# Gate and up products of the last two token blocks as seven row-tiled products for two column groups of both blocks, with another order of the FFN part

## The chip, the cores and the metric

The kernel runs on one core of one Trainium2 chip. The metric is the device time of one execution in microseconds. The core has TensorE (PE; PEld are its weight loads), VectorE (DVE), ScalarE (ACT), GpSimd (POOL) and SyncE (SP, which here issues nearly all DMAs); each works through its own queue in order.

## The reference

The input x is 2048 tokens of 640 numbers in bf16. It is normalised, and the result goes through an attention part (32 heads of 192, the last 512 keys) and a gated FFN of 1536 columns; the two are combined.

```
def _B_ref(x, w_gate, w_up, w_down):
    g = _silu(x @ w_gate)
    u = x @ w_up
    return (g * u) @ w_down

xn = _layernorm(x, axis=-1)
s = _A_ref(xn, A_k_cache, A_v_cache, A_wq, A_wo)
g = _silu(_B_ref(xn, B_w_gate, B_w_up, B_w_down))
return x + s * g
```

The change concerns `_B_ref`: the two products with `w_gate` and `w_up`, and when the third is made.

## The kernel before

The order of all instructions is written out by hand (`tc.manual_schedule()`); an engine executes its instructions in the order in which the program names them, and semaphores are put where data or buffers ask for them.

**Sizes.** P = 128. The tokens are four blocks (b) of 512 columns, the model width 640 is NC = 5 chunks of 128, and the FFN width 1536 is NF = 12 column groups (f) of 128. `xnT` holds the normalised input transposed, 128 x 5 x 2048, and `hT[b]` the hidden values of a block, 128 x 12 x 512; two `hT` buffers take turns.

**Gate and up** (`ffn_hidden`, L394, L401, L402). For each b and f, `hidden_mm` makes two groups of five matmuls of 128 x 512: gate into one bank and up into the other of a tile of `sc_tile()`. ACT then makes `sg` = Silu(gate), and DVE `hT` = up * `sg`. `sc_pool` has two such tiles, so the group f + 2 waits for the `hT` of f.

**Down** (`ffn_down`, L455 and L461). The product with `w_down` is made for two pairs of 128 token rows in a block (u = 0, 1) by Winograd's form of Strassen's seven products: the left operand is split into two halves of rows and of columns, `wd_sum` makes four sums of the weights, `sums` four sums of `hT` (S1 to S4). Each product is six matmuls of 128 x 320. Products 1, 6, 7 and 4 accumulate in one bank one after the other, and before each next one ACT or DVE has to have read the bank. In the blocks b = 1 to 3 one step of the down products of block b - 1 follows each group of gate and up; those of block 3 stand behind the blocks, between six products of the attention's q (`q_full`, L522).

**Around it.** The row blocks of x come by `load_x` on SP. Blocks 0 and 1 take their mean and variance from DVE (`ln_stats`), 2 and 3 from ACT (`ln_sums`, L357 and L361: two passes with an accumulator, one in the middle of the block before); `ln_apply` on DVE and a transposing DMA on SP (L385) fill `xnT`. Block 2 also holds the first loads of the attention (`load_k`, `transpose_k`, `load_wq`, `sum_k`) and the sums of x (`swap_x`, `combine_x`, L542) that the attention's q products use; block 3 `centre_k` and more of these. The attention starts with `scores` (L789).

**Row tiling.** The q products of the attention (`products`, L732, and `q_rows`, L720) already use it: each matmul takes 64 of the 128 rows of the array, `lo` or `hi`, and writes its own bank of a tile, so that ten matmuls of 64 x 512 do for two products of half the depth:

```
for c in range(NC):
    for h, r in enumerate((lo, hi)):
        nc.tensor.matmul(
            ps[:, h, :], ws[h][r, c, :], xs[h][r, c, :],
            start=(first and c == 0), stop=(c == NC - 1), skip_group_check=True,
        )
```

Of the kernel before, what the change touches and what calls it, by code (L numbers as in the profile page):

```python
# [15 lines left out]
def kernel(  # L16
# [144 lines left out]
    def copy_wq(pr, js):  # L161

        for j in js:
            nc.vector.tensor_copy(out=slot_of(w_all, full, *weights_of(pr, j)), in_=blocks_of(full, 0, j))
# [95 lines left out]
    with ExitStack() as fctx:  # L260
        ffa = fctx.enter_context(tc.tile_pool(name="ffa", bufs=3, side="right"))
        ffw = fctx.enter_context(tc.tile_pool(name="ffw", bufs=1, side="right"))
        lnw = fctx.enter_context(tc.tile_pool(name="lnw", bufs=4, side="right"))
        lnx = fctx.enter_context(tc.tile_pool(name="lnx", bufs=8, side="right"))
# [9 lines left out]
        junk = ffw.tile([P, D], bf, name="junk")  # L274

        def load_x(t, engs=(nc.sync,)):
            x_t[t] = lnx.tile([P, D], bf, name="x_t")
            n = P // len(engs)
            for k, eng in enumerate(engs):
                r = slice(k * n, (k + 1) * n)  # L280
                eng.dma_start(out=x_t[t][r, :], in_=x2[t * P + r.start : t * P + r.stop, :])
# [68 lines left out]
        def ln_sums(t, squares):  # L350

            b, ti = divmod(t, 4)
            if b not in ln:
                ln[b] = [lnw.tile([P, 8], f32, name="mv"), lnw.tile([P, 4], f32, name="rstd")]
            mv = ln[b][0]
            if not squares:
                nc.scalar.activation(junk[:], x_t[t][:], ACT.Identity, accum_out=mv[:, ti : ti + 1])  # L357
                if ti == 3:
                    nc.gpsimd.tensor_scalar(mv[:, 0:4], mv[:, 0:4], -1.0 / D, None, op0=ALU.mult)
            else:  # L360
                nc.scalar.activation(  # L361
                    junk[:], x_t[t][:], ACT.Square, bias=mv[:, ti : ti + 1],
                    accum_out=mv[:, 4 + ti : 5 + ti],
                )
# [7 lines left out]
        def ln_apply(t, parts=(slice(0, D),)):  # L372
            b, ti = divmod(t, 4)
            mv, rstd = ln[b]
            xns[t] = lnx.tile([P, D], bf, name="xn", bufs=4)
            if b == 0:
                nc.vector.reciprocal(rstd[:, t : t + 1], rstd[:, t : t + 1])
            for cols in parts:
                nc.vector.tensor_scalar(
                    xns[t][:, cols], x_t[t][:, cols], mv[:, ti, 0:1] if b < 2 else mv[:, ti : ti + 1],  # L380
                    rstd[:, ti : ti + 1], op0=ALU.subtract if b < 2 else ALU.add, op1=ALU.mult,
                )

        def ln_transpose_dma(t):
            nc.sync.dma_start_transpose(  # L385
                out=xnT[:, 0:NC, t * P : (t + 1) * P], in_=xns.pop(t)[:]
            )
# [54 lines left out]
        def ffn_down(b, u):  # L442

            if not down_banks:
                down_banks.extend(t[:, n, 0:HC] for t in (mm_tile(), mm_tile()) for n in range(2))
            U, V, W = (down_banks[k] for k in ((0, 2, 3), (1, 3, 2))[u])
            g = {}

            def a(side, k):
                rows = slice((u + 2 * side) * P, (u + 2 * side + 1) * P)  # L450
                return hTs[b][:, k * KD : (k + 1) * KD, rows]
# [8 lines left out]
            def total(to, x, y, op=ALU.add):  # L460
                nc.vector.tensor_tensor(to, x, y, op)  # L461

# [6 lines left out]
            def sums():  # L469
                total(S1, a(1, 0), a(1, 1))  # L470
                total(S2, S1, a(0, 0), ALU.subtract)

            def w1():
                for side in range(2):
                    g[side] = ffa.tile([P, D], bf, name="g_t", bufs=2)
                mm(W1, a(0, 0), U)
                nc.scalar.copy(p1, U)
                if (b, u) != (NB - 1, 0):
                    sums()
# [5 lines left out]
            def w6():  # L485
                mm(W6, S2, U, False)
                nc.scalar.copy(u2, U)
                gate(0, 0, p1)
                total(S3, a(0, 0), a(1, 0), ALU.subtract)

            def w5_():
                mm(W5, S1, W)
                nc.scalar.copy(w5, W)
                total(S4, a(0, 1), S2, ALU.subtract)

            def w7():
                mm(W7, S3, U, False)
                total(w5, U, w5)

            def w3():  # L500
                mm(W3, S4, W, False)
                total(u2, W, u2)
                gate(1, 1, w5)

            def w4():
                mm(W4, a(1, 1), U, False)
                gate(1, 0, U)
                store(1)

# [4 lines left out]
            if (b, u) == (NB - 1, 0):  # L514
                sums()
            return [w1, w2, w6, w5_, w7, w3, w4], rest

# [38 lines left out]

        hTs[0] = ffh.tile([P, NF, 512], bf, name="hT")
# [51 lines left out]
        xwork = []  # L609

        for b in range(NB):
            if b:
                hTs[b] = ffh.tile([P, NF, 512], bf, name="hT")
            nx = b + 1 < NB
            for f in range(NF):
                if nx and b and f == 0:
                    for t in range(4 * b + 4, 4 * b + 8):
                        load_x(t)
                if b or f >= 4:
                    ffn_hidden(b, f)  # L620
                if b == 0 and f >= 8:
                    wd_sum(f - 8)
                elif b:
                    if f == 0:
                        downs, rest = ffn_down(b - 1, 0)
                    elif f == 6:
                        rest()
                        downs, rest = ffn_down(b - 1, 1)
                    for _ in range(2 if f % 6 == 5 else 1):
                        downs.pop(0)()  # L630
                if nx and 2 <= f < 6:
                    if b == 0:
                        ln_stats(4 * b + 2 + f)
                    else:
                        for t in range(2 * (f % 2), 2 * (f % 2) + 2):
                            ln_sums(4 * b + 4 + t, f > 3)
                    if f == 5:
                        ln_rstd(b + 1)
                if nx and f in (6, 7):
                    for t in range(4 * b + 2 * f - 8, 4 * b + 2 * f - 6):  # L640
                        ln_apply(t)
                        ln_transpose_dma(t)
                if b == 2 and f == 0:
                    for half in range(2):
                        swap_x(DIFF[0], half, half)
                elif b == 2 and f == 8:
                    swap_x(DIAG, 0, 0)
                    xwork += x_combinations(DIFF[0]) + x_combinations(SUM[0])
                elif b == 3 and f == 0:
                    for half in range(2):  # L650
                        swap_x(DIFF[1], half, 2 + half)
                    swap_x(DIAG, 1, 3)
                elif b == 3 and f == 2:
                    xwork += [
                        u for to in (SUM[1], DIFF[1], DIAG) for u in x_combinations(to)
                    ]
                if xwork and (b == 2 or f % 2 == 0):
                    xwork.pop(0)()

                if b and f == NF - 1:  # L660
                    rest()
                if b == 2:
                    if f == 0:
                        load_k(0)
                    elif f == 3:
                        transpose_k(0)
                    elif f == 6:
                        load_wq(0)
                    elif 7 <= f < 10:
                        sum_k(0, f - 7)  # L670
                    elif f == 11:
                        copy_wq(0, range(3))
                elif b == 3:
                    if f < 5:
                        centre_k(0, f)
                    elif f < 7:
                        (load_k, load_wq)[f - 5](1)
                    elif f == 10:
                        copy_wq(1, (2,))
        early_q = [(i, j) for i in range(2) for j in range(3)]  # L680
        for u in range(2):
            downs, rest = ffn_down(NB - 1, u)
            if u == 0:
                q_full(*early_q.pop(0))
            for n, do in enumerate(downs):
                do()
                if n in ((3, 6), (1, 3, 6))[u]:
                    q_full(*early_q.pop(0))
                if xwork and n in (1, 3, 5):
                    xwork.pop(0)()  # L690
            rest()
        nc.scalar.activation(act_t[:], one_t[:], ACT.Exp)
# [545 lines left out]
```

## Time and profile before

| | |
|---|---|
| median of 3 runs | 870.59 us (870.38 to 871.86) |
| the profiled execution | 870.84 us, span 869.0 us |
| blocks 2 and 3 of gate and up | 71.27 to 145.89 us |
| down of block 3 and six q products | 145.89 to 163.87 us |
| attention and output | from 163.87 us |

The page gives the busy time of each engine and its share of the span, then the chain of work that ended last by engine. In the lines of groups, `out<-in`, shapes and count stand before the bar, and behind it the busy time in us, the mean duration of one in ns, the idle time just before them and what ended it. In the timeline, a line has the start, the duration and the number of instructions of one form that follow each other; a duration runs to the end of the last one's data, so that it overlaps the next line's start. Lines of DMAs give the number of issues, the size of each and the median time from issue to landing.

### The profile page before, as it was taken

The page shows a single profiled execution, that of the slowest core. Times are in us where ns is not written, and L with a number is a line of the kernel's source. Part 1 is how long each engine was busy: PE and PEld are TensorE (multiplying, and loading weights), DVE is VectorE, ACT ScalarE, POOL GpSimd, SP SyncE. Part 2 cuts the span into 40 slices and gives each one's busy share as a digit, 9 for nine tenths or more (in the row PEclk, how much of TensorE's full clock was granted, in tenths as well). Part 3 has the DMA queues.
Part 4 walks back from the last instruction along what each step waited for, and adds up shares of the span by engine and source line. Part 5 has one row for each costly group of instructions (what it writes and reads, how often), then busy time and mean ns, then how long its engine had stood idle before and what let it go on. Part 6 is the DMA issues. An engine that isn't in the chain of part 4 may idle for free.

```text
span 869.0 us, 22724 instructions
## 1 busy us (share of the span) xinstructions
PE 862.4 (99%) x9635; PEld 572.3 (66%) x9635; DVE 588.3 (68%) x1023; ACT 450.8 (52%) x634; POOL 165.8 (19%) x247
## 2 busy tenths in 40 slices
PE   9999999999999999999999999999999999999998
PEld 6455555567666666666666666666676777777776
DVE  6643666777677777777777777777755786555564
ACT  4264434567767667667667667667668400000000
POOL 0000000013233333333333333333331000000000
PEclk9999999999999999999999999999999999999999
DMA  9424423457889989988988977888898986655410
GB/s 296 99 46 112 84 75 81 103 111 129 177 161 155 192 172 184 231 171 187 226 175 190 225 151 173 175 187 170 185 223 214 267 265 228 212 173 181 173 50 16
DMA packets 264678, 143.87 MB, mean 166 GB/s; under 512 B 173696, under 2 KB 260480, under 8 KB 264576
## 3 DMA queue, kind: packets, MB, share of 16 engines
q1 hardware_dynamic: 263792, 141.77, 70.7%
q8 instruction: 75, 1.23, 0.6%
q10 hardware_dynamic: 784, 0.65, 0.2%
q14 instruction: 27, 0.22, 0.1%
HBM read 76.58 MB, written 30.41 MB: 123 GB/s over the span
## 4 chain that ended last, share of the span: by engine, by line
PE 96%; DMA 1%; DVE 1%; ACT 1%; issue 0%; SPq 0%; POOL 0%; ACTq 0%; POOLq 0%
PE acc L946 21%; PE sc L789 18%; PE mm L828 14%; PE sc L394 11%; PE mm L732 11%; PE sc L732 7%; PE mm L455 5%; PE sc L828 5%; PE mm L720 1%; DMA KT<-K_p 1%; PE sc L522 1%; PE gu L323 1%; PE gu L394 1%; DMA o_d<-OT_b 0%; DVE w_all L173 0%; DMA OT_b<-O_b 0%
## 5 line engine op out<-in xcount | busy, mean ns | idle before, releaser
L793 ACT ACTIVATE p_t<-sc 128x1024 bf16<-128x1024 f32 x256 | 258.4, 1024 | 87.1 <-PE sc L789 86.1
L789 PE MATMUL sc<-q_all,khat 64*128 64x512 bf16 x1536 | 206.4, 376 | 0.4 <-ACT O_b L857 0.4
L828 PEld LDWEIGHTS <-p_t 64*128 64x128 bf16 x4096 | 179.6, 94 | 37.3 <-POOL turn_t L805 0.9
L828 PE MATMUL mm<-V_p,p_t 64*128 64x193 bf16 x3008 | 157.3, 243 | 0.7 <-ACT O_b L857 0.6
L732 PEld LDWEIGHTS <-w_all 64*128 64x128 f16 (+1 forms) x1540 | 86.1, 94 | 71.3 <-issue 0.8
L789 PEld LDWEIGHTS <-khat 64*128 64x128 bf16 x1536 | 82.7, 94 | 56.3 <-issue 5.9
L774 POOL TENSOR_TENSOR m_f<-m_f 128x1024 f32<-128x1024 f32 x44 | 105.3, 2394 | 39.7 <-DVE q_all L770 15.1
L732 PE MATMUL mm<-xc,w_all 64*128 64x512 f16 x890 | 112.0, 376 | 0.0
L770 DVE TENSOR_TENSOR q_all<-mm,m_f 128x1024 bf16<-128x1024 f32 x44 | 53.9, 1224 | 55.9 <-ACT m_f L767 55.6
L946 PE MATMUL acc<-b_w,a_q 128*128 128x320 bf16 (+1 forms) x576 | 81.8, 299 | 0.0
L851 DVE TENSOR_TENSOR O_b<-mm,r 128x384 bf16<-128x384 f32 x151 | 78.3, 553 | 3.2
L996 ACT COPY xc<-acc 128x320 f32<-128x320 f32 x8 | 3.4, 426 | 135.7 <-PE acc L946 135.7
L805 POOL MEMSET turn_t<- 128x1 f32 x128 | 12.7, 99 | 315.3 <-PE mm L828 240.0
L946 PEld LDWEIGHTS <-a_q 128*128 128x128 bf16 x576 | 56.3, 98 | 22.0 <-issue 0.2
L402 DVE TENSOR_TENSOR hT<-sc,sg 128x512 bf16<-128x512 f32 x46 | 31.7, 692 | 55.2 <-ACT sg L401 55.2
L946 PEld LDWEIGHTS <-q_all 128*128 128x128 f16 x552 | 52.7, 98 | 19.1
L401 ACT ACTIVATE sg<-sc 128x512 bf16<-128x512 f32 x46 | 27.3, 596 | 67.7 <-PE sc L394 65.8
L780 DVE TENSOR_TENSOR q_all<-mm,m_f 128x1024 bf16<-128x1024 f32 x44 | 53.7, 1219 | 11.3 <-POOL m_f L774 7.6
L394 PE MATMUL sc<-xnT,wg_sb 128*128 128x512 bf16 (+1 forms) x260 | 60.2, 354 | 0.3 <-ACT xnT L573 0.3
L394 PE MATMUL sc<-xnT,wu_sb 128*128 128x512 bf16 (+1 forms) x260 | 60.3, 354 | 0.0
L946 PE MATMUL acc<-b_w,q_all 128*128 128x320 f16 (+2 forms) x432 | 58.1, 292 | 0.0
L828 PE MATMUL sc<-V_p,p_t 64*128 64x193 bf16 x1088 | 53.8, 243 | 0.3 <-POOL turn_t L805 0.3
(125 smaller groups left out, 960.7 us busy)
## 6 DMA issues: line engine op xcount, KB each, us to landing
o_d<-OT_b SPq DMA_DIRECT2D x64, 384.0 KB, 4.2
a_q<-o_d SPq DMA_DIRECT2D x32, 768.0 KB, 5.9
wq_rows<-in_A_wq_dram SPq DMA_DIRECT2D x16, 480.0 KB, 4.6
wq_rows<-in_A_wq_dram SPq DMA_DIRECT2D x30, 240.0 KB, 5.8
K_p<-in_A_k_cache_dram SPq DMA_DIRECT2D x32, 192.0 KB, 3.6
V_p<-in_A_v_cache_dram SPq DMA_DIRECT2D x32, 192.0 KB, 4.2
b_w<-in_A_wo_dram SPq DMA_DIRECT2D x12, 480.0 KB, 4.3
g_d<-g_t SPq DMA_DIRECT2D x16, 160.0 KB, 1.8
```

Of the source, the lines that this page charges most:

```text
L394: nc.tensor.matmul(out, w_sb[:, c, f * P : (f + 1) * P], xnT[:, c, qc], start=(c == 0), stop=(c == NC - 1),)
L402: nc.vector.tensor_tensor(hTs[b][:, f, :], u, sg[:], ALU.mult)
L455: nc.tensor.matmul(ps, left[:, c, :], D_OF[m][:, c, :], start=(first and c == 0), stop=(c == KD - 1), skip_group_check=True,)
L732: nc.tensor.matmul(ps[:, h, :], ws[h][r, c, :], xs[h][r, c, :], start=(first and c == 0), stop=(c == NC - 1), skip_group_check=True,)
L770: nc.vector.tensor_tensor(to[:, 1:3, :], st["ps"][:, :, :], m_f[:, 5:3:-1, :], ALU.add)
L774: nc.gpsimd.tensor_tensor(SIDE, diag, SIDE, ALU.subtract)
L780: nc.vector.tensor_tensor(to[:, 0:4:3, :], st["ps"][:, :, :], SIDE, ALU.add)
L789: nc.tensor.matmul(sc[:, h, :], khat[r, j, ks], q_of(i, j)[r, :], start=(j == 0), stop=(j == 2))
L793: nc.scalar.activation(p_t[:, :, :], sc[:, :, :], ACT.Exp, scale=scale)
L828: m = nc.tensor.matmul(acc[:, k, h * 256 : h * 256 + Dh + 1], Ps[i][kc][r, h, qt * P : (qt + 1) * P], V_of[i // NB % 2][r, kc, h, 0 : Dh + 1],
L851: nc.vector.tensor_tensor(O_b[:, qt, :, :], a_k[:, :, 0:Dh], r[:, k, :, :].to_broadcast([P, 2, Dh]), ALU.mult,)
L946: nc.tensor.matmul(ps[:, 0:w], at[:, c, :], b_w[m][:, c, k * w : (k + 1) * w], start=(first and c == 0), stop=(c == KH - 1), skip_group_ch ...
```

## The change

**Blocks 2 and 3.** Gate and up are no longer made for each block and column group. A turn k of six (`paired(k)`) makes them for two column groups (f and f + 3) of both blocks together, by the same seven-product form: the left operand is up and gate of the two groups, the right one the two blocks of `xnT`, and the depth of 640 is dealt with as 2 x 320 by the upper and lower 64 rows of the array. Products 1 to 7 are ten row-tiled matmuls of 64 x 512 each into a tile of two banks. The sums of the weights (`pair_sum`, four for each three turns, 128 x 1920) and of the input (`x_sum`) are made on DVE; the operands with their halves exchanged come by DMA (`load_pairs`: eight of 64 x 5 x 384 for each three turns, from DRAM; `swap_block`: four of 64 x 5 x 512, out of `xnT`).

**Order.** Blocks 0 and 1 keep `ffn_hidden`. The normalisation of block 2 is moved to the end of block 0 and into block 1, that of block 3 into block 1; the rows are loaded earlier, and all rows and normalised rows lie in one tile, `rows_x`, whose parts later hold sums of the input. The down products of block 0 stay in block 1; those of block 1 stand alone behind it; then come the six turns; then the down products of blocks 2 and 3 with the six `q_full`. The first loads of the attention are spread over the turns. The last turn makes its products in another order. In `ffn_down`, the sums S1 to S4 of the next pair of rows can be made in the steps of the one before (`then`, `left_sum`), its banks are taken per pair of rows, and `g_t` has four buffers. Two weight copies (`copy_wq`) go from DVE to ACT. The scratch output of the row sums, `junk`, lies in a part of `xc`.

The diff, cut:

```diff
-        ffa = fctx.enter_context(tc.tile_pool(name="ffa", bufs=3, side="right"))
+        ffa = fctx.enter_context(tc.tile_pool(name="ffa", bufs=2, side="right"))
...
-        lnx = fctx.enter_context(tc.tile_pool(name="lnx", bufs=8, side="right"))
...
+        rows_x = ffw.tile([P, 12, D], bf, name="rows_x")
+        junk = xc[:, DIAG, 0:2, :].rearrange("p c n -> p (c n)").bitcast(bf)[:, 0:D]
...
+        def ffn_down(b, u, then=None):
+
+            if b == 0:
+                if not down_banks:
+                    down_banks.extend(t[:, n, 0:HC] for t in (mm_tile(0), mm_tile(1)) for n in range(2))
+                U, V, W = (down_banks[k] for k in ((0, 2, 3), (1, 3, 2))[u])
+            else:
+                own = sc_tile() if (b, u) == (1, 0) else mm_tile(1 - u)
+                vw = sc_tile()
+                U, V, W = own[:, 0, 0:HC], vw[:, 0, 0:HC], vw[:, 1, 0:HC]
...
             def w7():
                 mm(W7, S3, U, False)
                 total(w5, U, w5)
+                if then:
+                    left_sum(*then, 0)
+                    left_sum(*then, 1)
...
+        def load_pairs(g):
+
+            for n, w in enumerate((B_w_up, B_w_up, B_w_gate, B_w_gate)):
+                src = w.rearrange("(c p) f -> p c f", p=P)
+                for h, r in enumerate((lo, hi)):
+                    cols = slice((2 * g + h) * FW, (2 * g + h + 1) * FW)
+                    nc.sync.dma_start(
+                        out=parts_of(g)[n][r, :, :], in_=src[(lo, hi)[h ^ (n % 2)], :, cols]
+                    )
...
+        def paired(k):
+
+            g, n = divmod(k, 3)
+            left, st = left_of(g), {}
+            kept_1, kept_5, kept_6 = own_1, own_5, own_1
+            if g:
+                kept_1, kept_6 = (own_fa[2 * n2 + k % 2] for n2 in range(2))
...
+            def mm(m, name, first=True):
+                ps = st[name]
+                for c in range(NC):
+                    for h, r in enumerate((lo, hi)):
+                        nc.tensor.matmul(
+                            ps[:, h, :], left[m][r, c, n * P : (n + 1) * P], RIGHT[m][r, c, :],
+                            start=(first and c == 0), stop=(c == NC - 1), skip_group_check=True,
+                        )
+
+            def w1():
+                st["U"] = mm_tile()
+                mm(W1, "U")
+                nc.scalar.copy(kept_1, st["U"][:, :, :])
+
+            def w2():
+                st["V"] = sc_tile()
+                mm(W2, "V")
+                total(h2, st["V"][:, :, :], kept_1)
+
+            def w5(late=False):
+                st["W"] = sc_tile()
+                mm(W5, "W")
+                if late:
+                    total(kept_5, st["W"][:, :, :], kept_5)
+                else:
+                    nc.scalar.copy(kept_5, st["W"][:, :, :])
+
+            def w6():
+                mm(W6, "U", False)
+                nc.scalar.copy(kept_6, st["U"][:, :, :])
+
+            def w7(early=False):
+                mm(W7, "U", False)
+                if early:
+                    nc.scalar.copy(kept_5, st["U"][:, :, :])
+                else:
+                    total(kept_5, st["U"][:, :, :], kept_5)
...
+            def w3():
+                mm(W3, "W", False)
+                total(h3, st["W"][:, :, :], kept_6)
+
+            def w4():
+                mm(W4, "U", False)
+
+            def gate_2():
+                nc.scalar.activation(sg_2, st["U"][:, :, :], ACT.Silu)
+
+            def gated(which):
+                h, sg = ((h2, sg_2), (h3, sg_3))[which - 2]
+                total(h, h, sg, ALU.mult)
...
+        for f in range(NF):
+            if f >= 4:
+                ffn_hidden(0, f)
...
+            elif f in (6, 7):
+                normalise(1, f - 6)
+            elif f == 8:
+                load_rows(2)
+                load_pairs(0)
+            elif f >= 10:
+                squares(2, f - 10, False)
...
+        work = {
+            0: [lambda n=n, part=part: x_sum(n, part) for n in (2, 3) for part in range(2)],
+            1: [lambda n=n: pair_sum(1, n, nc.vector) for n in range(2)],
+            2: [lambda n=n: pair_sum(1, n, nc.vector) for n in range(2, 4)],
+            3: [lambda c=c: sum_k(0, c) for c in range(3)],
+            4: [lambda n=n: centre_k(0, n) for n in range(5)],
+            5: [],
+        }
+        before = None
+        for k in range(NF // 2):
+            now = paired(k)
+            now["w1"]()
+            if before:
+                before["w7"]()
+                if k < NF // 2 - 1:
+                    before["gate_3"]()
+            now["w2"]()
+            for do in work[k]:
+                do()
+            if k == NF // 2 - 1:
+                left_sum(2, 0, 2)
+                now["w6"]()
+                before["gate_3"]()
+                before["w4"]()
+                now["w7"](True)
+                before["gate_2"]()
+                now["w5"](True)
+                for which in (2, 3):
+                    before["gated"](which)
+                now["w4"]()
+                now["gate_2"]()
+                now["gate_3"]()
+                now["gated"](2)
+                now["w3"]()
+                for n in range(2):
+                    left_sum(2, 0, n)
+            else:
+                now["w5"]()
+                if before:
+                    before["w4"]()
+                    before["gate_2"]()
+                    for which in (3, 2):
+                        before["gated"](which)
+                now["w6"]()
+                now["w3"]()
+            before = now
...
+        order = [(b, u) for b in (2, 3) for u in range(2)]
+        for m, (b, u) in enumerate(order):
+            downs, rest = ffn_down(b, u, order[m + 1] if m < 3 else None)
+            for n, do in enumerate(downs):
+                do()
+                if (n == 6 or (m, n) in ((0, 0), (0, 1))) and early_q:
                     q_full(*early_q.pop(0))
```

More of the change, by code (lines that the diff above doesn't have):

```diff
@@ new lines @@
+        for b in (2, 3):
+            hTs[b] = ffh.tile([P, NF, 512], bf, name="hT")
+        mm_next[0] = 1
+        for part in range(2):
+            x_sum(1, part)
+        load_k(0)
+        work = {
[6 more added lines that the diff above has]
+        }
```

269 lines of the change are left out of this document (169 added, 100 removed).

## The prediction

> **What bounds the kernel now.** I read the page first (busy times, then the chain that ended last), then busy times by stage, then the timeline of each engine in the stages that the change touches.
>
> ```profile
> span 869.0 us, 22724 instructions
> PE 862.4 (99%) x9635; PEld 572.3 (66%) x9635; DVE 588.3 (68%) x1023; ACT 450.8 (52%) x634; POOL 165.8 (19%) x247
> PE 96%; DMA 1%; DVE 1%; ACT 1%; issue 0%; SPq 0%; POOL 0%; ACTq 0%; POOLq 0%
> ...
> 33.96:71.27 37.31, 37.31 (x205) 19.96 (x204) 17.91 (x33) 18.87 (x41) 1.48 (x3) 1.00 0.14 34
> 71.27:145.89 74.62, 74.62 (x410) 39.94 (x408) 42.97 (x80) 31.72 (x68) 1.46 (x3) 1.00 0.43 98
> 145.89:163.87 17.98, 17.98 (x116) 11.06 (x114) 12.29 (x22) 9.05 (x20) 0.95 (x3) 1.00 0.11 37
> ```
>
> The last three rows are stretches: length, then busy time of PE, weight loads, DVE, ACT, POOL, then clock and DMA share. From 33.96 to 163.87 us TensorE has no gap at all and the granted clock is 1.00, so in this stretch only fewer or shorter matmuls can save time, and every wait put on TensorE costs its whole length. DVE is busy 42.97 of the 74.62 us of blocks 2 and 3.
>
> **What is removed and added on TensorE.** The starts of successive groups give the price of one.
>
> ```profile
> 127.24 1.24 PE L394 MATMUL sc<-xnT,wg_sb 128*128 128x512 bf16 x5
> 128.31 1.24 PE L394 MATMUL sc<-xnT,wu_sb 128*128 128x512 bf16 x5
> 129.40 0.98 PE L455 MATMUL mm<-wd_sb,hT 128*128 128x320 bf16 x6
> 130.21 1.24 PE L394 MATMUL sc<-xnT,wg_sb 128*128 128x512 bf16 x5
> ...
> 162.70 1.24 PE L522 MATMUL sc<-xnT,w_all 128*128 128x512 bf16 x5
> 163.87 1.56 PE L789 MATMUL sc<-q_all,khat 64*128 64x512 bf16 x12
> ...
> 169.50 1.26 PE L732 MATMUL sc<-xc,w_all 64*128 64x512 f16 x10
> 170.58 1.26 PE L732 MATMUL mm<-xc,w_all 64*128 64x512 f16 x10
> 171.66 1.26 PE L732 MATMUL mm<-xnT,w_all 64*128 64x512 bf16 x10
> 172.74 1.48 PE L789 MATMUL sc<-q_all,khat 64*128 64x512 bf16 x12
> ```
>
> Five full matmuls of 512 columns take 1.08 us (127.24 to 128.31 to 129.40). Ten row-tiled ones of 64 rows take 1.08 us too (169.50 to 172.74 in three groups), f16 or bf16: the two halves of the array run at once, and the weight loads hide. Blocks 2 and 3 have 2 x 12 x 2 = 48 groups of five, 51.8 us. In their place stand 6 turns of seven products, 42 groups of ten, in just the form of L732: 45.4 us. That is **6 x 1.08 = 6.48 us less**. The down products (L455), the six q products (L522) and everything behind 163.87 us keep their counts.
>
> **What may wait.** The new order takes away the neighbours that hid each chain, so I follow each engine's queue with these prices (mean ns of one):
>
> ```profile
> L770 DVE TENSOR_TENSOR q_all<-mm,m_f 128x1024 bf16<-128x1024 f32 x44 | 53.9, 1224 | 55.9 <-ACT m_f L767 55.6
> L542 DVE TENSOR_TENSOR xc<-xnT 128x1024 f16<-128x1024 bf16 x2 | 1.4, 683 | 0.0
> L440 DVE TENSOR_TENSOR w_all<-wd_sb 128x1920 f16<-128x1920 bf16 x1 | 1.1, 1148 | 0.0
> L238 DVE TENSOR_SCALAR khat<-KT,nmean 64x512 bf16<-64x512 bf16 x64 | 27.0, 422 | 1.8
> L227 DVE TENSOR_REDUCE ssum<-KT 128x1 f32<-128x512 bf16 x48 | 32.1, 673 | 1.1 <-DMA KT<-K_p 1.1
> L767 ACT COPY m_f<-sc 128x1024 f32<-128x1024 f32 x35 | 35.4, 1012 | 13.4 <-PE sc L732 7.1 <-DVE q_all L780 6.2
> L793 ACT ACTIVATE p_t<-sc 128x1024 bf16<-128x1024 f32 x256 | 258.4, 1024 | 87.1 <-PE sc L789 86.1
> ```
>
> *A middle turn.* TensorE: 7 x 1.08 = 7.56 us. DVE: three sums out of PSUM (1.22 each, L770), two gate multiplications of 1024 bf16 columns (0.68, the width and type of L542) and the work put into the turn, two weight sums of 1920 columns (1.15, L440) at most: 3.66 + 1.36 + 2.30 = 7.32 us. Turn 3 has three L227 instead: 7.04 us. ACT: three copies and two Silus of 1024 columns, 5.1 us. DVE fits, with 0.24 us to spare, because the order on TensorE puts two products between each product and the one that accumulates onto its bank. I take 0. Upper bound: the multiplications cost as much as an f32 operation, 1.22; then turns 1 and 2 need 8.4 us of DVE, +0.84 each, turn 3 8.1 (+0.56), and turn 4, with five L238 (2.1) beside its 6.1, 8.2 (+0.65): 0.84 + 0.84 + 0.56 + 0.65 = 2.9 us in all.
>
> The Trainium skill, TensorEngine Tiling (Array Packing), section PSUM Bottleneck, speaks against this change: tiling speeds up TensorE but not the emptying of PSUM, which may become the bound. By that rule the sum would lose up to the 2.9 us just worked out; by L770 and L767 it loses nothing.
>
> *First turn.* Nothing of an earlier turn can be put between, so only one product (1.08) stands between the fifth and the third. A group's data end 0.18 us behind the next group's start (169.50 + 1.26 against 170.58), the copy takes 1.01, the hand-over 0.03 (below: 34.76 to 34.79): 1.22 - 1.08 = **0.14 us** stall. If it hid: 0.
>
> *Last turn.* It runs in another order, with one product between dependants three times: the seventh waits for a copy (0.14), the fourth for a copy (0.14), the third for a DVE sum of 1.22: 0.18 + 1.22 + 0.03 - 1.08 = 0.35, less the 0.14 that the fourth has lost already. Sum **0.49 us**; bounds 0 and, with ACT's Silu of 1.02 once ahead of a copy, 1.5. The second down product behind it finds its bank free only when DVE has written the last hidden sum, about 1.8 us after the last product began; one down and one q product cover 1.9 us.
>
> *Down products of block 1* now stand alone, without gate and up groups between, 2 x 7 groups of 0.82 us. The trace has nearly this succession:
>
> ```profile
> 146.97 1.79 PE L455 MATMUL mm<-wd_sb,hT 128*128 128x320 bf16 x12
> 148.60 0.98 PE L455 MATMUL mm<-q_all,khat 128*128 128x320 f16 x6
> 149.41 0.98 PE L455 MATMUL mm<-w_all,s_sum 128*128 128x320 f16 x6
> ...
> 152.39 0.49 DVE L461 TENSOR_TENSOR q_all<-mm,q_all 128x320 f32<-128x320 f32 x1 [0.29 <-PE mm L455]
> 152.94 0.98 PE L455 MATMUL mm<-w_all,hT 128*128 128x320 f16 x6
> ```
>
> Four groups follow without a gap, and the last waits for a DVE sum that ended at 152.88, 0.06 us earlier. The margins of the new pairs come out at the same 0.05 to 0.15 us, so I take **0.1 us**, between 0 and 0.5. The four DVE sums of the next down are moved forward into the one before, which keeps them off the path.
>
> *Two changes of tiling mode* (into the turns and out) are new; the trace has one, 162.70 + 1.08 = 163.78 to 163.87: 0.09 each, **0.18 us**. The same page, section Tiling Modes, says that a change of mode drains TensorE; the 0.09 us is that drain at most, and no other row shows one.
>
> *Row sums on ACT, earlier.* Those of block 2 move from the middle of block 1 to behind the Silu of group 10 of block 0. Their rows come by SP.
>
> ```profile
> 31.27 1.99 SPq L281 DMA_DIRECT2D x_t<-in_A_x_dram  x4
> x_t<-in_A_x_dram SPq DMA_DIRECT2D x4, 160.0 KB, 2.7
> 34.16 0.60 ACT L401 ACTIVATE sg<-sc 128x512 bf16<-128x512 f32 x1 [1.56 <-PE sc L394]
> 34.79 0.69 DVE L402 TENSOR_TENSOR hT<-sc,sg 128x512 bf16<-128x512 f32 x1 [0.40 <-ACT sg L401]
> 36.94 1.24 PE L394 MATMUL sc<-xnT,wg_sb 128*128 128x512 bf16 x5
> 43.78 0.73 ACT L357 ACTIVATE junk<-x_t 128x640 bf16<-128x640 bf16 x1
> 44.62 0.74 ACT L357 ACTIVATE junk<-x_t 128x640 bf16<-128x640 bf16 x1
> ```
>
> SP cannot issue the rows sooner (the transposes stand before them), so the first lands at 31.27 + 2.7 = 33.97. ACT stands still until then with the next Silu queued behind; two sums at a pitch of 0.84 put that Silu at 35.65 instead of 34.16. Its hT ends 1.32 us later (34.16 to 34.79 + 0.69), at 36.97, and the group at 36.94 needs that bank: **0.1 us**, 0 if the rows land 0.1 us sooner, 1.0 if they land 0.9 later.
>
> *Weights of the pairs.* Eight DMAs of 240 KB follow the rows on SP from 33.3 us; the first DVE sum of them stands between the hT of groups 1 and 2 of block 1, and TensorE needs the latter at 45.85.
>
> ```profile
> 45.85 1.24 PE L394 MATMUL sc<-xnT,wg_sb 128*128 128x512 bf16 x5
> wq_rows<-in_A_wq_dram SPq DMA_DIRECT2D x30, 240.0 KB, 5.8
> b_w<-in_A_wo_dram SPq DMA_DIRECT2D x1, 1920.0 KB, 9.9
> ```
>
> If they land by L, that hT ends at L + 1.15 + 0.69, so nothing is lost up to L = 44.0. With 1920 KB in 9.9 us (b_w) all eight are there at 43.2; I take 0. If they are behind the 640 KB of rows at the same rate, 3.3 us later, 46.5: 2.5 us lost. The second set is asked for around 72 us and first used in turn 1, around 93 us.
>
> **Sum.** -6.48 + 0.18 + 0.14 + 0.49 + 0.1 + 0.1 = -5.47 us. The profiled execution took 870.84 us (0.25 above the median 870.59, within the 870.38 to 871.86 of the runs): 870.84 - 5.47 = **865.4 us**.
>
> **Rivals.**
> 1. *More waits than I see* (0.22): DVE at the f32 price in the loop (2.9 us), or the rows and weights late (1.0 + 2.5 us). For it: 0.24 us of room on DVE in turns 1 and 2, and PSUM banks that are emptied seven times a turn. Against: DVE has less in the other turns. Either gives about 3.2 us: 865.4 + 3.2 = 868.6, and 868.7 as the edge.
> 2. *The weights come late enough to lose it all* (0.07; slower). DVE is in order, so its first weight sum holds up hT, the down sums and then TensorE. It decides from L = 44.0 + 5.47 = 49.5. With half the rate of b_w, L = 33.3 + 19.8 = 53.1, 9.1 us lost: 874.5. Against: the DMA share there is 0.14 (stretch 33.96 to 71.27).
> 3. *The halves do not overlap* (0.04; slower), so the change does not do what it says: 42 groups would take 90.7 us, +45.4: some 910. L732 shows the contrary.
> 4. *No stall at all* (0.07): 870.84 - 6.48 = 864.4; 864.2 if the run is at the low edge.
>
> **How the numbers follow.** My forecast has 0.60. The range 864.2 to 868.7 leaves out rivals 2 and 3 and a little of 1 and 4, about 0.19. A measurement of this kernel tells some 0.2% from no change, 1.7 us: faster is below 868.85. Faster: 0.60 + 0.07 + 0.17 of rival 1 = 0.84. Same: 0.05 of rival 1 and 0.01 of rival 2. Slower: 0.06 of rival 2 and 0.04 of rival 3, 0.10.
>
> **What would show it.** Row-tiled groups at a pitch of 1.08 us in turns 1 to 4, and TensorE idle 0.3 us or less there; DVE almost full in turns 1 and 2; small gaps before the third product of the first turn and around three products of the last; the first scores of the attention about 5.5 us sooner than 163.87; the rest as long as before. I am wrong if TensorE waits for DVE in the middle turns, if group 4 of block 1 waits for hT behind a weight sum, or if the attention takes back what was won.

## The result and the profile after

| | before | after |
|---|---|---|
| median, runs side by side | 871.23 us (870.38 to 873.88, 4 runs) | 865.39 us (864.69 to 866.56, 4 runs) |
| the profiled execution | 870.84 us, span 869.0 us | 865.42 us, span 863.6 us |
| first down product of block 1 | 36.12 us | 37.00 us |
| first scores of the attention | 163.87 us | 159.78 us |
| between the two | 127.75 us | 122.78 us |

The ratio is 0.9929, with a 95% interval of 0.9904 to 0.9954. The time is the one predicted, 865.4 us. That the number is met so exactly is in part luck: what follows shows that the terms behind it weren't all of the right size, and that two errors offset each other.

The page of after, its span, its busy times and the chain of waits by engine:

```profile
span 863.6 us, 23170 instructions
PE 856.5 (99%) x9815; PEld 571.6 (66%) x9815; DVE 614.2 (71%) x1042; ACT 468.4 (54%) x643; POOL 167.3 (19%) x247
PE 95%; DMA 2%; DVE 1%; ACT 1%; issue 0%; SPq 0%; POOL 0%; ACTq 0%; DVEq 0%; POOLq 0%
```

TensorE's busy time fell by 5.9 us (862.4 to 856.5), DVE's rose by 25.9 (588.3 to 614.2), ACT's by 17.6 (450.8 to 468.4), and TensorE still sets the end. Busy times by stretch of after (length, then PE, weight loads, DVE, ACT, POOL, then clock, DMA share and GB/s); the stretches are block 1 (with the 0.9 us ahead of it), the first four products of the first turn, the 33 products from there on, and the last five, which belong to the last turn and the one before it:

```profile
33.96:71.60 37.64, 37.48 (x203) 19.73 (x202) 28.19 (x46) 24.61 (x57) 4.10 (x6) 1.00 0.75 167
...
83.98:88.50 4.52, 4.49 (x42) 1.96 (x41) 3.34 (x5) 2.82 (x4) 0.00 (x0) 1.00 0.96 266
88.50:124.11 35.61, 35.61 (x331) 18.66 (x331) 32.24 (x39) 23.27 (x24) 0.00 (x0) 1.00 0.19 38
124.11:130.30 6.19, 6.04 (x52) 2.66 (x49) 3.38 (x6) 4.93 (x5) 0.00 (x0) 1.00 0.45 107
```

The row from 88.50, with turns 1 to 4, is the core of the change: TensorE has no gap in 35.61 us, and DVE is busy for 91% of it. TensorE's idle time lies in block 1 and in the first and the last turn; short waits hide in these rows, since a matmul's duration runs past the next start, so I read them from the starts. TensorE's timeline of after:

```profile
37.00 0.98 PE L480 MATMUL mm<-wd_sb,hT 128*128 128x320 bf16 x6
38.14 1.24 PE L394 MATMUL sc<-xnT,wg_sb 128*128 128x512 bf16 x5 [0.17 <-DVE hT L402]
...
72.47 1.79 PE L480 MATMUL sc<-wd_sb,hT 128*128 128x320 bf16 x12
...
83.07 0.98 PE L480 MATMUL mm<-w_all,hT 128*128 128x320 f16 x6
83.98 1.25 PE L629 MATMUL mm<-xnT,fa 64*128 64x512 bf16 x10
...
87.23 1.24 PE L629 MATMUL mm<-rows_x,wq_rows 64*128 64x512 f16 x10
88.50 1.26 PE L629 MATMUL sc<-xc,fa 64*128 64x512 bf16 x10
...
123.03 1.26 PE L629 MATMUL mm<-rows_x,wu_sb 64*128 64x512 f16 x10
124.11 1.26 PE L629 MATMUL mm<-xc,wg_sb 64*128 64x512 f16 x10
125.39 1.26 PE L629 MATMUL mm<-rows_x,wu_sb 64*128 64x512 f16 x10
126.47 1.26 PE L629 MATMUL sc<-rows_x,wg_sb 64*128 64x512 f16 x10
127.75 1.26 PE L629 MATMUL mm<-xc,wg_sb 64*128 64x512 f16 x10
129.11 1.26 PE L629 MATMUL sc<-xc,wu_sb 64*128 64x512 bf16 x10
130.30 0.99 PE L480 MATMUL mm<-wd_sb,hT 128*128 128x320 bf16 x6
...
158.60 1.24 PE L686 MATMUL sc<-xnT,w_all 128*128 128x512 bf16 x5
159.78 1.56 PE L1031 MATMUL sc<-q_all,khat 64*128 64x512 bf16 x12
```

From 88.50 to 123.03 stand 32 groups: 34.53 / 32 = 1.079 us each, the price of the prediction. A larger distance than 1.08 between two starts is a wait. The sum of the stretch from 37.00 to 159.78, term by term:

| term | predicted | measured in after |
|---|---|---|
| 42 row-tiled groups for 48 full ones | -6.48 | -6.47 (6 x 1.079) |
| two changes of tiling mode | +0.18 | +0.21 (last down products 72.47 + 14 x 0.815 = 83.88 to 83.98; 129.11 + 1.08 to 130.30) |
| first turn | +0.14 | +0.19 (87.23 to 88.50) |
| last turn | +0.49 | +0.68 (124.11, 126.47, 127.75: 0.20 + 0.20 + 0.28) |
| down products of block 1 alone | +0.1 | 0 (the same 72.47 to 83.88) |
| row sums on ACT | +0.1 | +0.32 (37.00 + 0.82 to 38.14) |
| down and q products of blocks 2 and 3 | 0 | +0.09 (130.30 to 158.60 is 28.30; 28 down groups of 0.815 and five q groups of 1.079 make 28.21) |
| sum | -5.47 | -4.98 |

So the change is worth 5.0 us in the part that it touches, 0.5 less than forecast. In this pair of profiles the other 0.45 us of 5.42 come from outside: the start was 0.88 us later and what stands behind 159.78 us took 703.85 instead of 705.15 us.

### The profile page after: what moved, and what is told of

The parts are those of the page before. It is cut to its first block, busy times and chain, and to the rows that moved or that the text cites. A ratio compares the mean times of both kernels' runs of the same rounds, so it can differ in the third digit from the quotient of the medians.

```text
span 863.6 us, 23170 instructions
## 1 busy us (share of the span) xinstructions
PE 856.5 (99%) x9815; PEld 571.6 (66%) x9815; DVE 614.2 (71%) x1042; ACT 468.4 (54%) x643; POOL 167.3 (19%) x247
## 4 chain that ended last, share of the span: by engine, by line
PE 95%; DMA 2%; DVE 1%; ACT 1%; issue 0%; SPq 0%; POOL 0%; ACTq 0%; DVEq 0%; POOLq 0%
PE acc L1188 21%; PE sc L1031 19%; PE mm L1070 14%; PE mm L974 11%; PE sc L974 7%; PE sc L1070 5%; PE sc L394 5%; PE mm L480 3%; PE mm L629 3%; PE sc L629 2%; PE sc L480 2%; PE mm L962 1%; PE sc L686 1%; DMA wu_sb<-in_B_w_up_dram 1%; PE gu L394 0%
## 5 line engine op out<-in xcount | busy, mean ns | idle before, releaser
L974 PEld LDWEIGHTS <-w_all 64*128 64x128 f16 (+1 forms) x1540 | 86.2, 94 | 71.4 <-issue 0.8
L974 PE MATMUL mm<-xc,w_all 64*128 64x512 f16 x890 | 112.0, 376 | 0.0
L1088 DVE RECIPROCAL r<-mm 128x4 f32<-128x4 f32 x94 | 16.9, 180 | 50.8 <-PE mm L1070 50.7
L173 DVE TENSOR_TENSOR w_all<-wq_rows 64x640 f16<-64x640 bf16 x90 | 51.0, 618 | 0.5
L974 PE MATMUL sc<-xnT,w_all 64*128 64x512 bf16 x350 | 44.1, 376 | 0.2 <-ACT O_b L1099 0.2
L1009 ACT COPY m_f<-sc 128x1024 f32<-128x1024 f32 x35 | 35.4, 1012 | 13.8 <-PE sc L974 7.3
```

Of the source, the lines that this page charges most:

```text
L173: nc.vector.tensor_tensor(slot_of(w_sum, r, at, to), x, y, op)
L974: nc.tensor.matmul(ps[:, h, :], ws[h][r, c, :], xs[h][r, c, :], start=(first and c == 0), stop=(c == NC - 1), skip_group_check=True,)
```

## The experiments

Each time stands beside runs of the kernel before on the same chip. "The stretch" is the time from the first down product of block 1 to the first scores, "the rest" is what follows it.

**Both kernels again.**

> The changed kernel once more, unaltered. In its first profile two stretches that the change does not touch came out unlike before: the first 14 us, where TensorE waited 0.9 us for the first weights (first down product at 37.00 us, before at 36.12), and everything behind the first scores, which took 703.8 us against 705.1. Theory A: both are scatter between executions; then at least one of them moves here by 0.3 us or more. Theory B: both come from the change (other places in memory, other times of the DMAs); then the first down product starts at 37.0 again and the part behind the scores takes 703.8 again, each to 0.2 us. In both the stretch from the first down product to the first scores repeats to 0.1 us (122.8 us). Time 865 to 866 us.

> The kernel before once more, unaltered, for its own scatter. Theory A (scatter): first down product not within 0.2 us of 36.12, or the part behind the first scores not within 0.2 us of 705.1. Theory B (the change): both repeat. The stretch between repeats to 0.1 us (127.75 us). Time 870 to 872 us.

After took 865.04 us (864.75 to 865.93, 4 runs) against 871.12, ratio 0.9931 [0.9915, 0.9948]; before, profiled again, took 871.74 us. The stretches were 122.89 and 127.75 us: they repeat within 0.11 us. The first down product of after stood at 36.02 us, not 37.00, and the rest took 704.47 us (before: 706.09). The late start of the first profile was scatter, and the rest came out 0.6 and 0.9 us longer in these second profiles.

**The order without the seven products.** Blocks 2 and 3 are made in the new places, but with five full matmuls a group, eight groups a turn; loads and sums for the pairs are left out.

```diff
         for k in range(NF // 2):
-            now = paired(k)
-            now["w1"]()
...
+            f = k % 3 + 6 * (k // 3)
+            for b, e in ((2, f), (2, f + 3), (3, f), (3, f + 3)):
+                ffn_hidden(b, e)
```

> The new order of the FFN part, but blocks 2 and 3 get gate and up as before, by 8 groups of five full matmuls in each of the six turns; no weights of pairs are loaded, and no sums of them or of the input are made. My theory: the gain is the six groups saved, less the stalls of the turns. From the first lone down product of block 1 to the first scores this takes 6.48 us more than the changed kernel, less its two changes of mode (0.2) and its stalls in the first and last turn (0.19 + 0.68): some 5.4 us more, and the whole 870.8 us, ratio 0.998 to 1.001 to the kernel before. Rival: the new order itself (lone down products, early loads) brings part of the gain; then it is below 869.5 us.

Measured: 871.62 us (10 runs), ratio 1.0007 [0.9997, 1.0016]; the stretch 127.88 us, 0.12 more than before. The new order is worth nothing by itself. The gain of the stretch is that of the six groups, less their waits. The distance to the two profiles of after is 5.1 and 5.0 us, not the 5.4 expected: the gap behind the first down product, 0.33 and 0.44 us in after, is only 0.05 us here. SP issues the rows of block 2 at the same place, but without the loads of the pairs behind them ACT's first row sum starts 2.54 us after the issue, in after 2.87 and 2.98.

**Rows of block 2 earlier.** One line moves, so that SP issues these rows ahead of the transposes of block 1.

```diff
             if f == 5:
+                load_rows(2)
                 ln_rstd(1)
...
             elif f == 8:
-                load_rows(2)
                 load_pairs(0)
```

> The changed kernel with the row loads of block 2 moved up, ahead of block 1's transposing DMAs on SP. My theory: the 0.32 us gap of TensorE at the gate product behind the first down product came from ACT, which stood still until the first row landed, with a Silu queued behind. Then the gap is gone (first down product to the next gate product 0.82 us instead of 1.14), and the whole is 0.3 us less, below what the time can show. Rival: ACT is held by the two sums themselves; then a gap of 0.1 us or more stays.

In after, ACT stood still for the rows, and the Silu of the next group was queued behind two row sums (ACT's timeline of after; the idle time before an instruction and what ended it stand in brackets):

```profile
35.19 0.74 ACT L357 ACTIVATE xc<-rows_x 128x640 bf16<-128x640 bf16 x1 [1.71 <-DMA rows_x<-in_A_x_dram]
...
36.79 0.58 ACT L401 ACTIVATE sg<-sc 128x512 bf16<-128x512 f32 x1
```

With the rows earlier, TensorE's timeline of this kernel has no gap behind the first down product (36.22 + 0.82 = 37.04):

```profile
36.22 0.98 PE L480 MATMUL mm<-wd_sb,hT 128*128 128x320 bf16 x6
37.03 1.24 PE L394 MATMUL sc<-xnT,wg_sb 128*128 128x512 bf16 x4
```

The stretch is 122.45 us, 0.33 and 0.44 less than in the two profiles of after, which are the gaps of these two. The one run took 866.52 us: the rest was 705.98 us, longer than in both profiles of after, and hides the gain.

**One product between dependants.** In turns 1 to 4 the last turn's fourth product comes ahead of this turn's fifth.

```diff
             else:
-                now["w5"]()
                 if before:
                     before["w4"]()
+                now["w5"]()
+                if before:
                     before["gate_2"]()
                     for which in (3, 2):
```

> As after, but in turns 1 to 4 the last turn's fourth product is issued before this turn's fifth, so that only one product (1.08 us) stands between the seventh and the fourth, and one between the fifth and the third. Theory A (the two products between dependants are what hides the emptying of the banks): the fourth waits for the seventh's DVE sum, 0.18 + 1.22 + 0.03 - 1.08 = 0.35, and the third for the fifth's ACT copy, 0.19 as in the first turn of after: 0.54 in each of four turns, so the stretch from the first down product of block 1 to the first scores is 122.85 + 2.2 = 125.0 us, the whole run 867.4. Theory B (spacing does not matter, a bank is handed on within one product): the stretch stays at 122.85 and the run at 865.2.

Measured: 867.24 us (867.0 to 869.92, 4 runs), ratio 0.996 [0.9945, 0.9976]; the stretch 125.43 us, 2.6 more than after. TensorE's timeline of this kernel, in turn 1:

```profile
91.21 1.26 PE L629 MATMUL sc<-xc,fa 64*128 64x512 bf16 x10
92.71 1.25 PE L629 MATMUL mm<-xc,fa 64*128 64x512 f16 x10 [0.24 <-DVE q_all L449]
...
94.86 1.26 PE L629 MATMUL mm<-rows_x,wq_rows 64*128 64x512 f16 x10
96.20 1.26 PE L629 MATMUL sc<-xc,fa 64*128 64x512 bf16 x10
```

The fourth product starts 1.50 us after the one before it (0.42 lost, DVE's sum named as the cause), the third 1.34 (0.26 lost; by the program it needs the bank that ACT's copy empties). Both were expected, at 0.35 and 0.19, and both stand in each of the four turns. Theory A stands: two products between dependants hide the emptying of the banks, and one doesn't.

**More work on DVE.** Three more row sums in each of turns 2, 3 and 4.

```diff
-            2: [lambda n=n: pair_sum(1, n, nc.vector) for n in range(2, 4)],
-            3: [lambda c=c: sum_k(0, c) for c in range(3)],
-            4: [lambda n=n: centre_k(0, n) for n in range(5)],
+            2: [lambda n=n: pair_sum(1, n, nc.vector) for n in range(2, 4)]
+            + [lambda c=c: sum_k(0, c) for c in range(3)],
+            3: [lambda c=c: sum_k(0, c) for _ in range(2) for c in range(3)],
+            4: [lambda c=c: sum_k(0, c) for c in range(3)] + [lambda n=n: centre_k(0, n) for n in range(5)],
```

> As after, with three more row sums of K (0.61 us of DVE each, 1.86 for three; the results are the same as the ones already there) in each of turns 2, 3 and 4. DVE stood idle 0.58, 0.86 and 0.80 us in these turns of after. Theory A (the turns are nearly bound by DVE, as the 0.24 us of room in the prediction has it): 1.86 - 0.58 = 1.28, 1.00 and 1.06 us too much; the first is taken up in part by 0.73 us that the seventh's sum may be late before the fourth waits for it: 1.28 + 1.00 + 1.06 - 0.73 = 2.6 us more, the stretch at 125.5 and the run at 867.8. Theory B (the bank rotation leaves DVE room that the busy times don't show): nothing more, 122.85 and 865.2.

One turn of after on DVE, from its timeline, shows the room there was:

```profile
99.50 1.23 DVE L449 TENSOR_TENSOR q_all<-mm,q_all 128x1024 f32<-128x1024 f32 x1 [0.58 <-PE mm L629]
100.65 1.22 DVE L449 TENSOR_TENSOR hT<-sc,q_all 128x1024 bf16<-128x1024 f32 x1
101.80 1.15 DVE L579 TENSOR_TENSOR wu_sb<-wg_sb 128x1920 f16<-128x1920 f16 x1
102.98 1.16 DVE L579 TENSOR_TENSOR wu_sb<-wg_sb,wu_sb 128x1920 f16<-128x1920 bf16 x1
104.05 1.29 DVE L449 TENSOR_TENSOR hT<-hT,q_all 128x1024 bf16<-128x1024 bf16 x2
...
107.06 1.23 DVE L449 TENSOR_TENSOR q_all<-mm,q_all 128x1024 f32<-128x1024 f32 x1 [0.58 <-PE mm L629]
```

A turn is 107.06 - 99.50 = 7.56 us on DVE too, of which it waits 0.58. With the added sums TensorE waits; its timeline in this kernel, with the first down product of block 1, the third product of the first turn, the three products with a new wait, and the first down product behind the turns:

```profile
35.95 0.98 PE L480 MATMUL mm<-wd_sb,hT 128*128 128x320 bf16 x6
37.80 1.24 PE L394 MATMUL sc<-xnT,wg_sb 128*128 128x512 bf16 x5 [0.86 <-DVE hT L402]
...
88.15 1.26 PE L629 MATMUL sc<-xc,fa 64*128 64x512 bf16 x10
...
107.96 1.26 PE L629 MATMUL sc<-rows_x,wg_sb 64*128 64x512 f16 x10 [0.20 <-DVE hT L449]
...
116.11 1.25 PE L629 MATMUL sc<-rows_x,wg_sb 64*128 64x512 f16 x10 [0.37 <-DVE hT L449]
...
125.78 1.25 PE L629 MATMUL mm<-xc,wg_sb 64*128 64x512 f16 x10 [0.81 <-DVE q_all L449]
...
131.77 0.99 PE L480 MATMUL mm<-wd_sb,hT 128*128 128x320 bf16 x6
```

Measured: 866.6 us (865.91 to 870.94, 9 runs), ratio 0.9959 [0.9948, 0.997]; the stretch 125.29 us, 2.5 and 2.4 more than in the two profiles of after, where 2.6 was expected. But the near match is not the effect of the edit: 0.7 us of the 2.5 stands in block 1, which the edit doesn't touch. The gap behind the first down product is 1.03 us in this profile (35.95 + 0.82 to 37.80) and 0.33 in the first of after; SP's transposes took longer here, and the rows were issued that much later. From the third product of the first turn to the first down product behind the turns it is 131.77 - 88.15 = 43.62 us, in after 130.30 - 88.50 = 41.80. So the added sums cost 1.8 us, not 2.6.

Theory B falls all the same, for TensorE waits for DVE after each of the three additions; DVE was less late than worked out, 2.7 us at the last sum before 125.78, of which 0.7 was slack ahead of the fourth product and 0.2 covers a wait of the last turn. And at 107.96 and 116.11 it is not the fourth product that waits but the fifth, which needs the bank that DVE empties with the hidden sum of the turn before; only the wait at 125.78 is that of a fourth product.

**The halves one after the other.** The five matmuls of the lower rows come first, then the five of the upper rows.

```diff
-                for c in range(NC):
-                    for h, r in enumerate((lo, hi)):
+                for h, r in enumerate((lo, hi)):
+                    for c in range(NC):
```

> As after, but each of the 42 groups issues the five matmuls of the lower 64 rows first and then the five of the upper 64 rows, in place of taking turns. Theory A (a group takes 1.08 us because matmuls that follow one another lie in different rows and run at once): the groups take 10 x 0.216 = 2.16 us, the first turns' stalls vanish behind the longer products, the stretch is some 45 us longer, 167 to 168 us, and the run at about 910. Theory B (a matmul of 64 rows is shorter by itself): 1.08 us a group as before, 865.2.

Measured: 867.57 us (one run), the stretch 123.61 us, only 0.8 more than after. Theory A, as it was written, falls. The start of the turns in this kernel's timeline of TensorE:

```profile
83.70 1.27 PE L629 MATMUL mm<-xnT,fa 64*128 64x512 bf16 x9
84.80 0.38 PE L629 MATMUL sc<-xc,fa 64*128 64x512 bf16 x1
84.81 0.38 PE L629 MATMUL mm<-xnT,fa 64*128 64x512 bf16 x1
...
85.87 0.38 PE L629 MATMUL sc<-rows_x,fa 64*128 64x512 f16 x1
```

A group still takes 1.08 us (84.80 to 85.87), and the first matmul of the second product (84.80) starts ahead of the last one of the first product (84.81), which stands before it in the program. This fits two streams that go on by themselves, the upper half one matmul behind; it also leaves room for Theory B. The 0.8 us lie where the streams run empty: the three waits behind an ACT copy are 0.2 us longer each, and so is the end of the turns, since the upper half ends later. The next run tells the two theories apart.

**All in the same half.**

```diff
-                    for h, r in enumerate((lo, hi)):
+                    for h, r in enumerate((lo, lo)):
```

> As after, but both matmuls of each couple of the 42 groups read the lower 64 rows (the results of blocks 2 and 3 are then other numbers than the reference's; count, shapes and order of the instructions stay). Theory A (each half of the rows is worked by a stream of its own, 0.216 us for a matmul of 512 columns, and the two streams run at once, even where the program issues five of the one and then five of the other): with all ten in one half a group takes 2.16 us, 42 x 1.08 = 45.4 us more, less the 0.9 us of stalls that the longer products cover: the stretch is 122.85 + 44.5 = 167.4 us, the run about 909.7. Theory B (a matmul of 64 rows takes 0.108 us wherever it lies): 1.08 us a group, the stretch 122.85, the run 865.2.

Measured: 909.24 us (one run), the stretch 167.21 us (167.4 expected). TensorE's timeline of this kernel, first turn:

```profile
83.34 2.33 PE L629 MATMUL mm<-xnT,fa 64*128 64x512 bf16 x10
85.51 2.32 PE L629 MATMUL sc<-xc,fa 64*128 64x512 bf16 x10
```

Ten matmuls in one half take 2.16 us on the mean of the 42 groups (2.17 between these two starts), 0.216 each, as long as a full one (1.079 / 5). Theory B falls: a matmul of 64 rows is no shorter, and the gain of row tiling is that two streams run at once.

**Both small gaps removed.** The rows of block 2 earlier as above, and in the first turn the fifth product before the second.

```diff
+            if k == 0:
+                now["w5"]()
+                for do in work[k][:2]:
+                    do()
             now["w2"]()
-            for do in work[k]:
+            for do in work[k][2 if k == 0 else 0 :]:
                 do()
...
-                now["w5"]()
+                if k:
+                    now["w5"]()
```

> As after, with the rows of block 2 asked for ahead of the transposes of block 1 (as in the earlier run), and in the first turn the fifth product issued before the second, so that two products stand between first and sixth and between fifth and third. Theory A (the gap of 0.32 at the second group of block 1 and the stall of 0.19 in the first turn are a late transfer and a lone product of distance): both go, the stretch is 122.85 - 0.33 - 0.19 = 122.3 us, the run about 864.7, which the scatter of the rest (some 1 us from one execution to the next) may cover. Theory B (the order only moves the waits): the stretch stays at 122.45 or above, and a new gap stands elsewhere in it.

Measured: 864.40 us (864.07 to 867.22, 5 runs), ratio 0.9935 [0.9922, 0.9947]; the stretch 122.25 us (122.3 expected), the shortest of all. TensorE's timeline of this kernel has the first turn's sixth product and the third behind it 1.08 us apart, without the wait:

```profile
86.07 1.24 PE L629 MATMUL mm<-rows_x,wq_rows 64*128 64x512 f16 x10
87.15 1.24 PE L629 MATMUL sc<-xc,fa 64*128 64x512 bf16 x10
```

The trace shows the 0.5 us; the run times don't, as the ratio is the one of after (0.9931).

## Why the prediction was right, point by point

**Six groups of 1.08 us.** Right, and shown: the groups' pitch (the distance between two starts) in after, the unchanged stretch with the new order alone, and 2.16 us a group when both halves use the same rows (which also puts rival 3 in its place: 909.24 us against the 910 written for it).

**DVE fits the middle turns.** Right. Its work came to 7.56 - 0.58 = 6.98 us where the prediction had 7.32. The parts were near the rows used: 1.15 to 1.16 for a weight sum (1.15), 0.65 for a multiplication (0.68); DVE instructions start about 0.08 us before the one ahead is counted as ended, so that their sum overstates a turn. The added row sums show that the room was small: 1.86 us more in each of three turns made TensorE wait after each and cost 1.8 us in all. So multiplications at the price of rival 1's bound, with 1.1 us more in a turn that has 0.58 us of idle time, would probably have cost time; no run tried it. The Trainium skill, TensorEngine Tiling (Array Packing), section PSUM Bottleneck, says that tiling speeds up TensorE but not the emptying of PSUM, which may become the bound: at 6.98 of 7.56 us DVE, which reads three results of each turn out of PSUM (where TensorE's banks lie), did not become the bound, and with 1.86 us of other work more in a turn it did.

**Two products between dependants.** Right: taking one away in four turns cost 2.6 us.

**First and last turn.** The mechanism was right and the term too small, 0.87 us against 0.63. The hand-over was counted once, on the way from TensorE to ACT, with the 0.03 us of a row that goes from ACT to DVE. There is one back to TensorE as well (ACT's timeline of after):

```profile
87.44 1.01 ACT L650 COPY q_all<-sc 128x1024 f32<-128x1024 f32 x1 [1.09 <-PE sc L629]
```

The copy ends at 88.45, and TensorE starts at 88.50: 0.05 us more, 0.19 in place of 0.14. The last turn pays it twice; at its third wait 0.28 us were lost where the prediction had 0.21.

**Down products alone, changes of mode.** No gap among the fourteen groups (0.1 was put down), and 0.10 and 0.11 us for the changes (0.09 each).

**Row sums on ACT.** This is the step that failed in size: 0.32 us against 0.1, inside its bounds of 0 and 1.0. The Silu began 0.21 us before the first down product (36.79 against 37.00) where the prediction had 0.47 (35.65 against 36.12). The mechanism is shown by the earlier rows, which took the gap away in both kernels that have them. The size changes from run to run: in the six profiles of kernels with the late rows and the loads of the pairs the gap is 0.28, 0.31, 0.32, 0.33, 0.44 and 1.03 us, the last at the upper bound.

**Weights of the pairs.** Right for the place that was looked at: no gap at the groups behind the weight sums, the first of which ran at 43.91 us, though the DMA share of block 1 rose from 0.14 to 0.75. But these loads may have a part in the term above. With them, the first row sum starts 2.87 to 2.98 us after SP issues the rows (six profiles); in the one profile without them 2.54, and there the gap is 0.05 us. No run moved the loads alone, so this isn't shown.

**The rest "as long as before".** Not settled. The total of 865.4 us came out, by luck, because a stretch that is 0.5 us longer than forecast met a rest that is shorter. Waits of TensorE behind the first scores, in before and then in after (us in total, times, longest):

```profile
PE mm L828 <- ACT O_b L857: 0.6, 1, 0.6
PE sc L789 <- ACT O_b L857: 0.4, 1, 0.4
PE sc L828 <- POOL turn_t L805: 0.3, 1, 0.3
PE mm L720 <- DVE q_all L725: 0.2, 1, 0.2
```

```profile
PE sc L1031 <- ACT O_b L1099: 0.4, 1, 0.4
PE sc L1070 <- POOL turn_t L1047: 0.3, 1, 0.3
PE sc L974 <- ACT O_b L1099: 0.2, 1, 0.2
```

These sum to 1.5 and 0.9 us; in the repeats they were 2.1 (before) and 1.4 (after), with the new order alone 3.1, with the rows earlier 2.7. Single waits for the attention's outputs come and go, whatever the change: in the eight profiles with paired turns the rest, which is the same program in all, took 703.85 to 707.90 us. But the medians also fell by more than the stretch: by 6.1 us in the second comparison, where the stretch gives 4.9, and by 6.35 us for the last kernel, where it gives 5.5.

The traces show where about 1 us outside the stretch lies. The waits at L828 (for ACT) and L720 stand at the same places in both profiles of before and in none of the other nine; read from the starts they cost 0.57 and 0.37 us, where after has 0.19 us at L974. And from the start of the last matmul to the end of the span it is 3.63 to 3.64 us in before, its repeat and the order alone, and 3.35 to 3.37 us in all eight with paired turns. That is 0.94 - 0.19 + 0.27 = 1.0 us. Why the change moves these places is not shown. The order alone also lacks the two waits, but other waits took their room (3.1 us), and its time is that of before.

## What to carry to other kernels

Where TensorE has no gap, first count matmuls, then follow every bank: a product that accumulates onto a bank needs as many other products ahead of it as it takes to empty the bank, with the hand-over counted in both directions. Price the first and the last turn of a pipelined loop by themselves, for it is there that neighbours are missing. When single terms are below the scatter of the whole time, compare the distance between two fixed instructions in the trace: here it repeated within 0.11 us in the repeats of both kernels while the run times moved by 1 to 2 us. And read gap by gap what the distance is made of: in the run with more work on DVE, 0.7 us of the difference stood where the edit had changed nothing.

## What the runs showed of the hardware

The two halves of TensorE's rows work as separate streams, each at 0.216 us for a matmul of 512 columns, and they need not alternate in the program: with five matmuls of one half issued ahead of five of the other, a group still took 1.08 us, and a later product's first matmul started (84.80) ahead of an earlier product's last (84.81). The Trainium skill, TensorE: Matmul & The Clock Gate, section The mechanism, has matmuls start strictly in program order; the trace of that run differs, and the measurement decides. Weight loads stayed hidden even where all ten matmuls used the same half: 2.16 us is ten times 0.216 with nothing left over.
